# A delta-rule attention with a feed-forward behind it: T kept by columns in the head, and four moves of copies, loads and steps

## The chip, the cores and the metric

The kernel runs on one core of one Trainium2 chip. The metric is the device time of one execution in microseconds, as the median of several runs. TensorE (PE in the profile; PEld is its loading of weights), VectorE (DVE), ScalarE (ACT), GpSimd (POOL) and SyncE (SP, which here only issues DMAs) each work through a queue of their own, in order, and wait for one another by semaphores.

## What is computed

A linear attention with a delta rule runs over 768 steps for 4 sequences of 8 heads with 48 entries each. Its output, 3072 tokens of 384 entries, goes through a feed-forward layer of 2048 columns with a leaky ReLU.

```python
for t in range(S):
    y[:, :, t] = einsum('bhd,bhde->bhe', q_t, state)
    v_old = einsum('bhde,bhd->bhe', state, k_t)
    state = state + beta_t * einsum('bhd,bhe->bhde', k_t, v_t - v_old)
...
h = x @ w_in            # 384 -> 2048
g = maximum(0.01 * h, h)
out = g @ w_out         # 2048 -> 384
```

Here k_t is k divided by its norm.

## The kernel before, in words

The 768 steps are cut into 12 blocks of 64. Within a block the recurrence is a triangular system. `gram` makes the products of keys with keys and with queries, `inv` inverts the triangular matrix by elimination, `solve` puts its halves together (`merge_z`, tiles pz and zs; `merge_u`, tile pu, results in rt) and gets y from it (`step_w`, `step_y`, tile ys). `columns` turns y into x, and `ffn` runs the feed-forward of a block over 16 columns f of 128 hidden entries: the first products of f and f + 1 (tile ph, line 800), an activation on ScalarE, and PD = 2 columns later the second product (tile po, line 791). Heads and sequences are split into two groups g = 0, 1.

The inverses of blocks 0 and 1 are made together, ahead of everything else (`inv(0)`, where `two` is true): T is one tile of 32 by 32 entries on 128 partitions, T[p, m, i] with rows m. Step j of `eliminate` adds T[m, j] * L[j, i] to T[m, i] for all m up to j and all i behind j. Where both sides have more than ONE = 3, it does so with two products into tmp (line 407) and two sums (line 412), one pair for the even rows and one for the odd rows; else with single instructions (line 395). Behind the last step VectorE transposes T twice in blocks of 32 by 32: into tc (line 466), whose parts `place` copies into rt (line 516), and in place (line 472), from where `merge_u` takes it for blocks 0 and 1. `place(0, g, 1)` runs on ScalarE, `place(0, g, 0)` on VectorE.

Beside this, in the head, the weights come in eight loads of 1.5 MB (`load_w`, tile wr, tags w0 to w7). Each is taken apart into parts that TensorE multiplies: `pack` on ScalarE (line 148), `conv` on VectorE (lines 158 to 161), `expand` on ScalarE (line 168), `final` on VectorE (line 175). Block 0 works in plain 32 bits (`w32`), later blocks in two parts each (`cast`, `lows`).

What sets the order: a library plans each engine's order from a simulated timeline, and the kernel binds it where it matters. `behind(name)` puts an instruction behind the one last marked with that name on its engine. The mark `dv` chains the weight conversions on VectorE one behind the other, so that `final` of weight 1 comes behind `conv` of weight 2; `po` puts pz and pu of later blocks behind the last second product. From line 850 on generators are woven into the loop over f: SV[n] lists for block n the columns f behind which the next block's solve goes a step on, IV and G4 the same for its inverse and its Gram. `warm` keeps TensorE busy with products that nobody reads.

The inputs of block 2's Gram (tile kq, line 288, four DMAs of 192 KB on SP's queue) are asked for in the head. The inverse of block 3 goes to memory as tt and comes back as the tile sq (line 495), which pz of block 3 reads.

Of the kernel before, what the change touches and what calls it, by code (L numbers as in the profile page):

```python
# [9 lines left out]
F32 = mybir.dt.float32  # L10
# [5 lines left out]
ALU = mybir.AluOpType  # L16
# [4 lines left out]
D = 48  # L21
# [4 lines left out]
GS = 2  # L26
NGR = NSEQ // GS
# [3 lines left out]
HS = H * NSEQ  # L31
HC = C // 2
P = 128
# [10 lines left out]
R0 = 64  # L44
# [3 lines left out]
def delta_moe_kernel(ctx: ExitStack, tc, kq0, kqT, kv, qT, beta, cst, w_all, out, nblk):  # L48
# [73 lines left out]
    def behind(name):  # L122

        return tc.issue_after(mark[name]) if name in mark else nullcontext()
# [155 lines left out]
    def gram(n):  # L280
        need(sv, "y", n - Q_BUFS // NGR)
        kqs = []
        for g in range(NGR):
            t = sb.tile([P, GS, NPAIR, 2, C], F32, tag="kq", name=f"kq{n}_{g}", bufs=KQ_BUFS)
            kqs.append(t)
            with behind("L" if n > BG + 1 else "kq"), behind("A" if BG + 1 < n < 2 * BG + 2 else None):
                for b in range(2):
                    nc.sync.dma_start(t[b * R0:b * R0 + D].rearrange("p s u x t -> p (s u x t)"), kqT[n, g, b])
        if n == GS:
            yield  # L290
        b0 = where[n][0]
        Lh[b0] = sb.tile([P, HC, HC], F32, tag="L", name=f"L{b0}", bufs=2)
        gd = dr.tile([64, HC, HC], F32, tag="gd", name=f"gd{n}")
        queue = nc.gpsimd if n == GS * NGR else nc.sync
        for g in range(NGR):
            kq = kqs[g]
            gs = sb.tile([P, 2, NPAIR, C], F32, tag="gs", name=f"gs{n}_{g}", bufs=2)
            if not g:
                gm[n] = sb.tile([P, GU, HC], F32, tag="gm", name=f"gm{n}", bufs=GM_BUFS)

            ps = [ps_a.tile([P, 512], F32, tag="a", name=f"pg{n}_{g}_{b}") for b in range(2)]
            pv = [x.rearrange("p (u x t) -> p x u t", u=NPAIR, x=2) for x in ps]
            for p in range(NPAIR):
                for c in range(2):
                    for b in range(2):
                        r = slice(b * R0, b * R0 + D)
                        with behind("ph") if n > 2 else nullcontext():
                            nc.tensor.matmul(ps[b][c * 64:(c + 1) * 64, p * 128:(p + 1) * 128],  # L308
                                             kq[r, c ^ b, p, 0], kq[r, c ^ b, p].rearrange("p x t -> p (x t)"),
                                             start=True, stop=True)  # L310
            for b in range(2):
                nc.scalar.copy(gs[:, b], pv[b][:, 0])  # L312
            for c in range(2):
                for e in range(2):
                    a = e * HS + g * GH + c * GU
                    queue.dma_start(
                        gd[a:a + GU].rearrange("l j i -> j l i"),
                        gs[c * 64 + e * HC:c * 64 + (e + 1) * HC].rearrange("p b u t -> p (b u) t")[:, :, e * HC:(e + 1) * HC])

            def masked(pv=pv, qa=of("q", n, g), to=DATA[g]):  # L320
                for b in range(2):
                    for c in range(2):
                        r = slice(c * 64, (c + 1) * 64)
                        with behind("gl") if n > 2 else nullcontext():
                            nc.vector.tensor_tensor(  # L325
                                qa[to, c, b * NPAIR:(b + 1) * NPAIR], pv[b][r, 1],
                                tri[r].rearrange("p (o t) -> p o t", o=1).broadcast_to([C, NPAIR, C]), ALU.mult)

            def corners(g=g, gs=gs):
                for c in range(2):  # L330
                    k = 2 * g + c
                    with behind("h") if n > 2 else nullcontext():
                        (nc.scalar.copy if n > 2 else nc.vector.tensor_copy)(gm[n][k * HC:(k + 1) * HC].rearrange("p (b u) t -> p b u t", b=2), gs[c * 64:c * 64 + HC, :, :, HC:])

            if n == 2:
                masked()
                corners()
            elif not g:
                masked()
                held.append(corners)  # L340
            else:
                tails.extend([[masked], held + [corners]])
                held.clear()
            if g == NGR - 1:
                for r in range(2):
                    i = queue.dma_start(Lh[b0][r * 64:(r + 1) * 64].rearrange("l j i -> l (j i)"), gd.rearrange("l j i -> l (j i)"))
                if n == GS * NGR:
                    mark["kq"] = i.ins
                if n > GS:
                    mark["L"] = i.ins  # L350
                done.add((gram, n))
            yield
# [32 lines left out]
    def eliminate(b, L, j, T, m):  # L385


        w = HC - 1 - j
        gate = "xl" if b == 1 and j >= XL else None
        if min(m, w) <= ONE:  # L390
            rows = m <= w
            for x in range(min(m, w)):
                with behind(gate):
                    t = T[:, x, j + 1:] if rows else T[:, 0:m, j + 1 + x]
                    d = nc.vector.scalar_tensor_tensor(  # L395
                        t, L[:, j, j + 1:] if rows else T[:, 0:m, j],
                        T[:, x, j:j + 1] if rows else L[:, j, j + 1 + x:j + 2 + x], t, ALU.mult, ALU.add)
                mark["steps"] = mark[f"step{min(x, 1)}"] = d.ins
            return
        parts = []  # L400
        for x in range(min(m, 2)):
            t = T[:, x:m:2]
            k = t.shape[1]
            tv = sb.tile([P, 144], F32, tag=f"tmp{x}", name=f"tmp{b}_{j}_{x}", bufs=1)
            tv = tv[:, 0:k * w].rearrange("p (x w) -> p x w", x=k)
            with behind(gate):
                nc.vector.tensor_tensor(  # L407
                    tv, t[:, :, j:j + 1].broadcast_to([P, k, w]),
                    L[:, j, j + 1:].rearrange("p (o w) -> p o w", o=1).broadcast_to([P, k, w]), ALU.mult)
            parts.append((tv, t[:, :, j + 1:]))  # L410
        for x, (tv, t) in enumerate(parts):
            mark["steps"] = mark[f"step{x}"] = nc.vector.tensor_tensor(t, t, tv, ALU.add).ins  # L412
# [11 lines left out]
    def inv(b):  # L424
# [34 lines left out]
        for j in range(HC - 1):  # L459
            eliminate(b, L, j, T, j + 1 if two else j // 2 + 1)  # L460
            if two and j in WARM:
                warm(WARM[j], T[:, 0, j:j + 1])
            if j == HC - 2:
                if two:
                    Tc = sb.tile([P, HS, HC], F32, tag="L", name="tc", bufs=2)
                    nc.vector.transpose(Tc.rearrange("p l i -> p i l"), T.rearrange("p m i -> p i m"))

                    for i, n in enumerate(NB[b]):
                        Tts[n] = Tc, T[i * 64:i * 64 + HC]
                    for g in range(NGR):  # L470
                        place(0, g, 1)
                    d = nc.vector.transpose(T, T)
                    mark["inverse"] = d.ins
                    for g in range(NGR):
                        d = place(0, g, 0)
# [37 lines left out]
    def place(n, g, e):  # L513
        a = n * 64 + e * HC
        with behind("h" if n else "inverse"):
            return (nc.scalar.copy if e or n else nc.vector.tensor_copy)(
                half_of(n, g, e), Tts[n][0][a:a + HC].rearrange("p (y g u) i -> p g y u i", y=2, g=NGR)[:, g])

    squares = {}
# [117 lines left out]
    def solve(n):  # L637
# [88 lines left out]
        def step_y(g):  # L726

            qa, v = of("q", n, g), of("v", n, g)
            pv = ps_a.tile([P, 512], F32, tag="a", name=f"py{n}_{g}")
            for c, u, e in quarters():  # L730
                a = (c ^ (u // NPAIR)) * C + e * HC
                nc.tensor.matmul(pv[a:a + HC, u * D:(u + 1) * D], qa[:, c, u, e * HC:(e + 1) * HC], v[:, c, u], start=True, stop=True)  # L732
            ys[n, g] = y = sb.tile([P, DO], F32, tag="ys", name=f"ys{n}_{g}", bufs=3)
            mark["ys"] = nc.scalar.copy(y, pv[:, 0:DO]).ins
            if not n and not g:
                expand(0, "ys", slice(1, 2))

        slots = NSLOT - (n < EARLY)
# [158 lines left out]
    conv(1)  # L897
    expand(0, "rv", lo)
    final(0, lo)
    for j in (4, 5):  # L900
        load_w(j, "dv")
    weave(1, (sv, 2, 0, 1))
    next(gg)
    final(0, hi)
    work = {
        0: ((expand, 1, "xh"), (conv, 2)),
# [24 lines left out]


WEARLY, NPACK, NG = 4, 3, 5
WARM, FILL = {HC // 2: 28, HC - 2: 12}, dict(pz=2, pu=3)
KA = 2
BG = 2
ONE = 3
XL, IL = 24, HC - 1 - 24
IV, GG = ((9, 16), (6, 17), (2, 12), (2, 12)), ((2, 4), (1, 2))
G4 = (0, 1), (13, 14), (12, 13)  # L940
SV = (1, 2, 4, 5, 7, 12, 13), (4, 6, 7, 9, 11, 12), (2, 4, 5, 7, 9, 10), (3, 3, 5, 6, 8, 10, 11)
PD, FB = 2, 4


# [64 lines left out]
```

## Time and profile before

| | us |
|---|---|
| median of 3 runs | 593.85 |
| lowest, highest | 591.87, 595.17 |
| the profiled execution, time | 597.18 |
| the profiled execution, span | 595.4 |

| engine | busy us | share of the span |
|---|---|---|
| TensorE, matmuls | 565.9 | 95% |
| TensorE, weight loads | 520.0 | 87% |
| VectorE | 421.7 | 71% |
| ScalarE | 336.7 | 57% |
| GpSimd | 82.3 | 14% |

The profile is of one execution. Its times count from the start of the span. Busy shares are means over stages with different limits; the stages are told apart below by their time: the head up to 54 us, block 0's feed-forward up to 110, block 1's up to 162, and from there some 44 us for a block. The granted clock is that of TensorE: 1.00 is 2.4 GHz, 0.50 is 1.2 GHz.

### The profile page before, as it was taken

What the parts mean: (1) busy time and instruction counts of PE and PEld (TensorE: products, weight loads), DVE (VectorE), ACT (ScalarE), POOL (GpSimd) and SP (SyncE); (2) the same over time, 40 slices, a digit from 0 to 9 for tenths busy, and PEclk for the clock granted to TensorE, in tenths of its full rate; (3) what the DMA queues carried; (4) which work ended last, traced back from release to release, by engine and by line L of the source; (5) the groups of instructions that cost most, each with busy time, mean ns of one, the idle gap of its engine ahead of it and who ended that gap; (6) DMA issues with size and microseconds to landing.
All of it is one profiled execution on the core that took longest, in us unless ns stands there. A gap on an engine that the chain in (4) does not pass through costs nothing.

```text
span 595.4 us, 22234 instructions
## 1 busy us (share of the span) xinstructions
PE 565.9 (95%) x9137; PEld 520.0 (87%) x9137; DVE 421.7 (71%) x1788; ACT 336.7 (57%) x865; POOL 82.3 (14%) x143
## 2 busy tenths in 40 slices
PE   4588999989989999999999999999999999999996
PEld 4467777779879999999999999999999999999996
DVE  3998899969829769669669669579589489241221
ACT  3686989885536546545545545545555554454432
POOL 7000000130320030130310310310300400400100
PEclk9998999999989999999999999999999999999999
DMA  5994952272760390490590590591581640510101
GB/s 113 309 303 169 299 153 53 64 144 51 141 109 13 61 192 21 78 200 4 86 193 3 104 175 19 81 183 29 87 165 30 103 95 3 84 36 3 28 0 28
DMA packets 102502, 59.68 MB, mean 100 GB/s; under 512 B 90496, under 2 KB 91584, under 8 KB 101376
## 3 DMA queue, kind: packets, MB, share of 16 engines
q1 hardware_dynamic: 96992, 50.06, 39.0%
q0 software_dynamic: 4832, 7.48, 5.6%
q8 instruction: 72, 1.18, 0.9%
q10 hardware_dynamic: 576, 0.72, 0.6%
q14 instruction: 30, 0.25, 0.2%
HBM read 46.96 MB, written 11.27 MB: 98 GB/s over the span
## 4 chain that ended last, share of the span: by engine, by line
PE 74%; DVE 10%; ACT 7%; DMA 4%; issue 2%; SPq 1%; DVEq 0%; ACTq 0%
PE ph L800 29%; PE po L791 29%; PE pw L695 3%; ACT rv L630 2%; PE py L732 2%; PE pg L308 2%; DVE T L412 2%; DVE tmp L407 2%; PE pk L669 2%; PE pc L669 1%; PE px L767 1%; ACT cg L148 1%; DVE T L395 1%; DMA sq<-tt 1%; PE pz L534 1%
## 5 line engine op out<-in xcount | busy, mean ns | idle before, releaser
L791 PE MATMUL po<-w,gh 128*128 128x384 f32 x704 | 178.1, 343 | 0.0
L815 DVE TENSOR_TENSOR gl<-ph,gh 128x256 fp32r<-128x256 f32 x176 | 74.4, 423 | 139.7 <-ACT ph L814 136.3
L810 ACT ACTIVATE gh<-ph 128x256 fp32r<-128x256 f32 (+1 forms) x192 | 73.7, 385 | 175.9 <-PE ph L800 106.9
L800 PE MATMUL ph<-xh,w 128*128 128x256 f32 x1056 | 157.1, 285 | 0.0
L800 PEld LDWEIGHTS ph<-xh,w 128*128 128x128 f32 x1056 | 142.1, 191 | 4.1 <-issue 3.3
L791 PEld LDWEIGHTS po<-w,gh 128*128 128x128 f32 x704 | 120.4, 189 | 4.0 <-issue 1.6
L791 PE MATMUL po<-w,gl 128*128 128x384 f32 x352 | 112.2, 338 | 0.9 <-DVE gl L815 0.8
L800 PE MATMUL ph<-xl,w 128*128 128x256 f32 x528 | 91.0, 284 | 0.0
L412 DVE TENSOR_TENSOR T<-T,tmp 128x48 f32<-128x48 f32 (+12 forms) x490 | 87.8, 215 | 0.3
L407 DVE TENSOR_TENSOR tmp<-T,L 128x48 f32<-128x48 f32 (+12 forms) x490 | 87.5, 215 | 0.2
L800 PEld LDWEIGHTS ph<-xl,w 128*128 128x128 f32 x528 | 75.3, 192 | 0.3 <-issue 0.2
L791 PEld LDWEIGHTS po<-w,gl 128*128 128x128 f32 x352 | 65.3, 188 | 2.1 <-DVE gl L815 2.1
L814 ACT ACTIVATE ph<-ph 128x256 f32<-128x256 f32 x176 | 66.8, 380 | 0.0
L495 POOL DMA_DIRECT2D sq<-tt x36 | 21.2, 596 | 301.4 <-PE po L791 110.8
L842 POOL DMA_DIRECT2D out<-ob x44 | 23.3, 535 | 142.9 <-ACT ob L841 142.5
L325 DVE TENSOR_TENSOR rq<-pg,csb 64x256 f32<-64x256 f32 x80 | 33.8, 422 | 2.5 <-ACT gs L312 0.9
L680 ACT ACTIVATE rt<-pk 48x512 f32<-48x512 f32 x44 | 26.1, 593 | 6.4 <-PE pk L669 5.0
L697 ACT COPY rv<-pw 64x384 f32<-64x384 f32 x48 | 22.8, 475 | 3.5 <-PE pw L695 2.3
L791 PE MATMUL po<-cg,gh 128*128 128x384 f32 x64 | 23.1, 494 | 0.0
L800 PE MATMUL ph<-x,cg 128*128 128x256 f32 x96 | 22.3, 382 | 0.4 <-ACT x L772 0.4
L630 ACT ACTIVATE rv<-rv,nt 64x48 f32<-64x48 f32 x96 | 22.3, 318 | 0.2
L395 DVE SCALAR_TENSOR_TENSOR T<-L,T 128x27 f32<-128x27 f32 (+3 forms) x126 | 22.2, 242 | 0.0
(110 smaller groups left out, 657.6 us busy)
## 6 DMA issues: line engine op xcount, KB each, us to landing
wr<-in_w_all SPq DMA_DIRECT2D x8, 1536.0 KB, 13.8
kq<-in_kqT SPq DMA_DIRECT2D x40, 192.0 KB, 5.8
rv<-in_kv SPq DMA_DIRECT2D x24, 192.0 KB, 5.6
rk<-in_kv SPq DMA_DIRECT2D x24, 192.0 KB, 5.1
rq<-in_qT SPq DMA_DIRECT2D x24, 192.0 KB, 3.6
L<-gd SPq DMA_DIRECT2D x18, 256.0 KB, 4.4
out<-ob POOLq DMA_DIRECT2D x44, 96.0 KB, 4.4
td<-T SPq DMA_DIRECT2D x20, 128.0 KB, 3.2
```

The source lines that it names most:

```text
L325: nc.vector.tensor_tensor(qa[to, c, b * NPAIR:(b + 1) * NPAIR], pv[b][r, 1], tri[r].rearrange("p (o t) -> p o t", o=1).broadcast_to([C, NP ...
L395: d = nc.vector.scalar_tensor_tensor(t, L[:, j, j + 1:] if rows else T[:, 0:m, j], T[:, x, j:j + 1] if rows else L[:, j, j + 1 + x:j + 2 + ...
L407: nc.vector.tensor_tensor(tv, t[:, :, j:j + 1].broadcast_to([P, k, w]), L[:, j, j + 1:].rearrange("p (o w) -> p o w", o=1).broadcast_to([P ...
L412: mark["steps"] = mark[f"step{x}"] = nc.vector.tensor_tensor(t, t, tv, ALU.add).ins
L630: d = nc.scalar.mul(v[DATA[g], c, u], v[DATA[g], c, u], nt[DATA[g], g, c, u:u + 1])
L680: d = nc.scalar.mul(ts[g][STATE[g], c], pv[g][c * C:c * C + D].rearrange("p (y v) t -> p y v t", y=2), -1.0)
L791: i = nc.tensor.matmul(po[t][:, :DO], a[:, ts_], w, start=(f == 0 and k == 0), stop=(f == NFC - 1 and k + 1 == len(ways)))
L800: i = nc.tensor.matmul(ph, w[:, cc * P:(cc + 1) * P], a, start=(k == 0), stop=(k + 1 == len(ways)))
L810: i = nc.scalar.activation(gh, ph, AF.Prelu, alpha=0.01)
L814: i = nc.scalar.activation(ph, ph, AF.Prelu, alpha=0.01)
L815: mark["gl"] = mark[f"gl{n}_{f}"] = nc.vector.tensor_tensor(gl, ph, gh.bitcast(F32), ALU.subtract).ins
L842: nc.gpsimd.dma_start(out[r0:r0 + C], ob[a:a + C])
```

## The change

T of blocks 0 and 1 is kept by columns, T[p, i, m], and `eliminate` splits its columns m into a lower and an upper half in place of even and odd rows. The first transpose now reads T straight, the second reads it strided and writes into a tile of its own, G, which takes the place of weight 7 (tag w7). `place(0, 0, 1)` goes from ScalarE to VectorE, and the second transpose is put behind it. The second batch of warm matmuls has 7 in place of 12.

The loads of kq for block 2 wait for a copy of one column of ys into their tile, on GpSimd, and the mark `kq`, behind which weights are loaded, is on the last of them; the call that issues them and the loads of weights 4 and 5 change places accordingly. The second half of weight 0 is expanded behind y of g = 1, and no longer behind that of g = 0. SV[2], the steps of block 3's solve in block 2, becomes that of the later blocks without its first entry.

```diff
@@ gram
+            if n == GS:
+                nc.gpsimd.tensor_copy(t[:, 0, 0, 0, 0:1], ys[0, g][:, 0:1])
             with behind("L" if n > BG + 1 else "kq"), ...:
                 for b in range(2):
-                    nc.sync.dma_start(t[b * R0:b * R0 + D]..., kqT[n, g, b])
+                    i = nc.sync.dma_start(t[b * R0:b * R0 + D]..., kqT[n, g, b])
+            if n == GS:
+                mark["kq"] = i.ins
@@ eliminate
         parts = []
-        for x in range(min(m, 2)):
+        if not b:
+            for x, (lo, hi) in enumerate(((0, (m + 1) // 2), ((m + 1) // 2, m))):
+                tv = sb.tile([P, 144], F32, tag=f"tmp{x}", name=f"tmp{b}_{j}_{x}", bufs=1)
+                tv = tv[:, 0:(hi - lo) * w].rearrange("p (w x) -> p w x", w=w)
+                nc.vector.tensor_tensor(
+                    tv, T[:, j:j + 1, lo:hi].broadcast_to([P, w, hi - lo]),
+                    L[:, j, j + 1:].rearrange("p (w o) -> p w o", o=1).broadcast_to([P, w, hi - lo]), ALU.mult)
+                parts.append((tv, T[:, j + 1:, lo:hi]))
+        for x in range(min(m, 2) if b else 0):
@@ inv
-                    nc.vector.transpose(Tc.rearrange("p l i -> p i l"), T.rearrange("p m i -> p i m"))
+                    nc.vector.transpose(Tc.rearrange("p l i -> p i l"), T)
+                    G = sb.tile([P, 8 * DO], F32, tag="w7", name="turned", bufs=1)[:, 0:HC * HS].rearrange("p (m l) -> p m l", m=HC)
 
                     for i, n in enumerate(NB[b]):
-                        Tts[n] = Tc, T[i * 64:i * 64 + HC]
-                    for g in range(NGR):
-                        place(0, g, 1)
-                    d = nc.vector.transpose(T, T)
+                        Tts[n] = Tc, G[i * 64:i * 64 + HC]
+                    mark["placed"] = place(0, 0, 1).ins
+                    place(0, 1, 1)
+                    with behind("placed"):
+                        d = nc.vector.transpose(G, T.rearrange("p i m -> p m i"))
@@ place
-            return (nc.scalar.copy if e or n else nc.vector.tensor_copy)(
+            return (nc.scalar.copy if n or e and g else nc.vector.tensor_copy)(
@@ step_y
-            if not n and not g:
+            if not n and g:
                 expand(0, "ys", slice(1, 2))
@@ the order of the head
+    weave(1, (sv, 2, 0, 1))
+    next(gg)
     for j in (4, 5):
         load_w(j, "dv")
-    weave(1, (sv, 2, 0, 1))
-    next(gg)
@@ constants
-WARM, FILL = {HC // 2: 28, HC - 2: 12}, dict(pz=2, pu=3)
+WARM, FILL = {HC // 2: 28, HC - 2: 7}, dict(pz=2, pu=3)
-SV = ..., (2, 4, 5, 7, 9, 10), (3, 3, 5, 6, 8, 10, 11)
+SV = ..., (3, 5, 6, 8, 10, 11), (3, 3, 5, 6, 8, 10, 11)
```

Left out are the lines that only rename T's entries for the new order, in the single instructions of `eliminate` and in `warm`.

## Rows read from the trace of the kernel before

**Rows 1.** Busy time by stretch: stretch, length, busy (instructions) by engine, granted clock, DMA share, GB/s

```profile
36.67:58.12 21.45, 18.05 (x467) 14.36 (x468) 20.81 (x30) 15.34 (x28) 0.00 (x0) 0.84 0.63 184
...
54.00:110.00 56.00, 55.67 (x804) 42.09 (x805) 51.02 (x142) 51.11 (x93) 0.00 (x0) 1.00 0.61 180
...
172.00:173.00 1.00, 1.00 (x4) 1.00 (x4) 0.13 (x1) 0.83 (x3) 0.00 (x0) 0.50 1.46 130
...
175.00:176.00 1.00, 1.00 (x10) 1.00 (x8) 0.00 (x0) 0.00 (x0) 0.00 (x0) 0.83 0.00 0
...
210.00:254.00 44.00, 44.00 (x730) 41.64 (x729) 33.55 (x159) 23.16 (x62) 7.15 (x14) 1.00 0.50 96
```

**Rows 2.** Timeline of VectorE in the head: start, time, engine, line, operation, tiles, shapes, count

```profile
24.40 0.48 DVE L407 TENSOR_TENSOR tmp<-T,L 128x126 f32<-128x126 f32 x2
24.80 0.48 DVE L412 TENSOR_TENSOR T<-T,tmp 128x126 f32<-128x126 f32 x2
...
34.92 0.33 DVE L412 TENSOR_TENSOR T<-T,tmp 128x56 f32<-128x56 f32 x2
35.28 1.35 DVE L395 SCALAR_TENSOR_TENSOR T<-T,L 128x29 f32<-128x29 f32 x6
36.67 2.31 DVE L466 STREAM_TRANSPOSE tc<-T 128x1024 f32<-128x1024 f32 x1
39.09 1.25 DVE L472 STREAM_TRANSPOSE T<-T 128x1024 f32<-128x1024 f32 x1
40.36 0.86 DVE L516 COPY rt<-tc 32x512 f32<-32x512 f32 x2
...
56.36 1.75 DVE L175 SCALAR_TENSOR_TENSOR cg<-wr,cg 128x1536 uint32<-128x1536 uint32 x1
```

**Rows 3.** Timeline of TensorE, head and block 0

```profile
36.50 2.97 PE L421 MATMUL warm<-neg 128*128 128x512 f32 x12
...
58.60 2.86 PE L800 MATMUL ph<-x,cg 128*128 128x256 f32 x12
...
76.32 2.12 PE L584 MATMUL pu<-zs,T 32*32 32x32 f32 x64
```

**Rows 4.** Timeline of ScalarE, head and block 0

```profile
35.67 4.56 ACT L148 COPY cg<-wr 128x1536 bf16<-128x1536 bf16 x3
40.25 1.26 ACT L516 COPY rt<-tc 32x512 f32<-32x512 f32 x2
...
51.96 0.84 ACT L168 CAST cg<-cg 128x768 f32<-128x768 bf16 x1
...
62.80 1.61 ACT L148 COPY cg<-wr 128x1536 bf16<-128x1536 bf16 x1
...
91.54 1.67 ACT L148 COPY cg<-wr 128x1536 bf16<-128x1536 bf16 x1
```

**Rows 5.** Timeline of TensorE around its waits for sq, in brackets idle time before, and releaser

```profile
125.80 0.64 PE L534 MATMUL pz<-sq,gm 128*32 128x128 f32 x16 [1.56 <-DMA sq<-tt]
...
167.09 0.86 PE L791 MATMUL po<-w,gh 128*128 128x384 f32 x4
...
171.19 0.64 PE L534 MATMUL pz<-sq,gm 128*32 128x128 f32 x16 [2.89 <-DMA sq<-tt]
171.77 1.53 PE L791 MATMUL po<-w,gh 128*128 128x384 f32 x4
```

**Rows 6.** VectorE's groups by shape from 9 to 13 us: busy, mean ns, idle before

```profile
L250 DVE STREAM_TRANSPOSE L<-S 128x1024 f32<-128x1024 f32 x1 | 1.9, 1933 | 0.1
```

**Rows 7.** Timeline of SP's queue: issue, time to issue, count

```profile
24.77 7.01 SPq L288 DMA_DIRECT2D kq<-in_kqT  x4
...
65.17 0.33 SPq L133 DMA_DIRECT2D wr<-in_w_all  x1
```

**Rows 8.** Loads of weights, issue to landing: of 4 and 5, then of 7

```profile
DMA to landing us min/median/max: 6.1/8.8/11.6
...
DMA to landing us min/median/max: 15.2/15.2/15.2
```

More of the change, by code (lines that the diff above doesn't have):

```diff
@@ L285, in gram @@
             kqs.append(t)
+            if n == GS:
+                nc.gpsimd.tensor_copy(t[:, 0, 0, 0, 0:1], ys[0, g][:, 0:1])
             with behind("L" if n > BG + 1 else "kq"), behind("A" if BG + 1 < n < 2 * BG + 2 else None):
                 for b in range(2):
-                    nc.sync.dma_start(t[b * R0:b * R0 + D].rearrange("p s u x t -> p (s u x t)"), kqT[n, g, b])
+                    i = nc.sync.dma_start(t[b * R0:b * R0 + D].rearrange("p s u x t -> p (s u x t)"), kqT[n, g, b])
+            if n == GS:
+                mark["kq"] = i.ins
         if n == GS:
@@ L393, in eliminate @@
                 with behind(gate):
-                    t = T[:, x, j + 1:] if rows else T[:, 0:m, j + 1 + x]
+                    at = (lambda m, i: T[:, i, m]) if not b else (lambda m, i: T[:, m, i])
+                    t = at(x, slice(j + 1, HC)) if rows else at(slice(0, m), j + 1 + x)
                     d = nc.vector.scalar_tensor_tensor(
-                        t, L[:, j, j + 1:] if rows else T[:, 0:m, j],
-                        T[:, x, j:j + 1] if rows else L[:, j, j + 1 + x:j + 2 + x], t, ALU.mult, ALU.add)
+                        t, L[:, j, j + 1:] if rows else at(slice(0, m), j),
+                        at(slice(x, x + 1), j) if rows else L[:, j, j + 1 + x:j + 2 + x], t, ALU.mult, ALU.add)
                 mark["steps"] = mark[f"step{min(x, 1)}"] = d.ins
@@ L461, in inv @@
             if two and j in WARM:
-                warm(WARM[j], T[:, 0, j:j + 1])
+                warm(WARM[j], T[:, j, 0:1])
             if j == HC - 2:
@@ L940 @@
 G4 = (0, 1), (13, 14), (12, 13)
-SV = (1, 2, 4, 5, 7, 12, 13), (4, 6, 7, 9, 11, 12), (2, 4, 5, 7, 9, 10), (3, 3, 5, 6, 8, 10, 11)
+SV = (1, 2, 4, 5, 7, 12, 13), (4, 6, 7, 9, 11, 12), (3, 5, 6, 8, 10, 11), (3, 3, 5, 6, 8, 10, 11)
 PD, FB = 2, 4
```

## The prediction

> **What bounds the kernel now.** I read the busy time by stretch first [rows 1]. From 54 to 110 us TensorE is busy for 55.67 of 56.00 us, and from 210 on for all of 44.00: there every microsecond counts one for one, and nothing that ScalarE, VectorE or a DMA gains is worth anything. What can be won lies in the head, before TensorE runs without a gap, and in the stalls between. So two places matter. In the head I read VectorE's stretch from the first transpose to the last weight conversion before the second pair of first products: 20.81 of 21.45 us busy in 30 instructions [rows 1]. That is not an engine that waits. Its timeline [rows 2] ends this stretch with the final step of weight 1, 56.36 + 1.75 = 58.11; TensorE starts the products that read this weight at 58.60 [rows 3]. VectorE has 0.5 us of slack there, no more. ScalarE in the same head [rows 4] does three weight copies (35.67 + 4.56 = 40.23) and then, in the order of its queue, the two copies of rt at 40.25, though the first transpose had ended at 36.67 + 2.31 = 38.98. So the way through rt is held by ScalarE, and not by T. The second place is block 2 [rows 5]: pz of block 3 waits 2.89 us, from 168.30 to 171.19, for the DMA that fills sq, and after it the granted clock stands at 0.50, the 1.2 GHz level, until about 175.3 (the slice 175 to 176 shows 0.83) [rows 1].
>
> **T by columns, the elimination.** The number of instructions and of elements is the same: a step with m columns of T and w entries still makes two products and two sums of about m*w/2 elements. Runs of 28 and of 4 elements cost the same already (56 elements in 0.33 us a pair at the end of the loop [rows 2], 0.34 at its start), so I cost the new order of elements at nothing. What is new is who waits for whom. Before, rows of T were split into even and odd, and a row never changed its half; each instruction depends on the one two places ahead. Now the columns are split in the middle, and the middle moves: if m is even, the first half of the next step takes over one column of the second half of this one. Its product then reads what the instruction directly ahead has written. The price of that stands in [rows 2]: a pair that depends on nothing directly ahead starts 0.08 us before the earlier pair has ended (24.40 + 0.48 against 24.80), one that does starts 0.03 after (34.92 + 0.33 against 35.28). That is 0.11 us each, for m = 4, 6, ..., 26, twelve times: 1.3 us. Bounds: 0, if something can be put between, and 1.4.
>
> **The two transposes.** The first one reads and writes T strided by 128 bytes and takes 2.31, the second reads and writes without stride and takes 1.25 [rows 2]; the one of the start, strided reading alone, took 1.93 [rows 6]. Now the first reads straight and writes strided, which no row shows: between 1.25 and 2.31; I take 1.25 + (2.31 - 1.93) = 1.63. The second reads strided and writes straight, as the row with 1.93; bounds 1.25 and 2.31. Sum 3.56 before and 3.56 after, with bounds of -1.06 and +1.06.
>
> **rt's copy for one g on VectorE.** VectorE gets one copy more, 0.86 / 2 = 0.43 and 0.02 between [rows 2]: +0.45. ScalarE loses one of two, 1.26 / 2 = 0.63 [rows 4], and as that way starts at 40.25 whatever T does, pz for the second g starts 0.6 us earlier. The transpose into the new tile stands behind this copy on VectorE, but pu, its reader, needs zs first and has that cover.
>
> **The rest of the head.** The half of w that moves behind y of the second g is a cast of 0.84 on ScalarE [rows 4] that stands ahead of that y now: up to 0.84 won on the way to px, I take 0.6. Five of the twelve warm matmuls go, 5 x 2.97 / 12 = 1.2 us [rows 3]; they end ahead of pz in both kernels, so nothing. The four kq loads, asked for at 24.77 so far, and 7.01 us on SP's queue [rows 7], go behind a one-column copy on POOL that waits for ys. On SP they hold what is queued behind them: the loads of weights 4 and 5. Of these the first landed 6.1 us after its issue [rows 8], at 58.9, and ScalarE reads it at 62.80 [rows 4]. With four issues of 0.3 to 0.5 us and 0.8 MB ahead of it I reckon with 61 to 62: covered, with under 2 us to spare. If that cover went, ScalarE's queue would stand. The tile for the turned T has the place of weight 7, so that this load waits until pu of block 1 has read it, 76.32 + 2.12 = 78.4 [rows 3] in place of 65.17 [rows 7]; with the 15.2 us it took [rows 8] it lands by 93.6 at the latest, and with 6.1 us, for a queue as empty as weight 4 found it, by 84.5. Its reader starts at 91.54 [rows 4]. I take the early end, since 65 to 78 has been cleared of it, so nothing.
>
> **Sum for the head.** TensorE's and ScalarE's side gains 0.6 + 0.6 = 1.2. VectorE's side loses 1.3 + 0 + 0.45 = 1.75: the final step of weight 1 ends at 59.9, the products behind it start there, and not at 58.60: **+1.3 us**. With no slack up to 110 it stays.
>
> **Block 3's solve a step later.** In block 2, pz stands behind the second product of one more column, as long as the one that began at 167.09 and ended at 168.30: 1.2 us at most, 1.0 without its start. The DMA comes when it comes (its chain begins in block 1), so of 2.89 some 1.0 is filled and 1.9 us stay. The wait of 1.56 us at 125.80 [rows 5] left the granted clock at 1.00, so I take it that the clock stays up. Four matmuls of po took 1.53 us behind the stall and 0.86 ahead of it [rows 5]; over the 3.4 us to 175.3 this is 3.4 x (1 - 0.86 / 1.53) = 1.5. Together **-2.5 us**; bounds -1.0 (the clock falls all the same) and -4.4 (no wait left).
>
> **The whole** is +1.3 - 2.5 = -1.2 us. The profiled execution had a span of 595.4 and a time of 597.18, 3.3 above the median of the three runs; I apply the difference to the median: 593.85 - 1.2 = **592.6 us**. By the bounds of this case alone 590.9 to 594.5.
>
> **Rivals.** *The dependence costs nothing* (0.17). The wait is hidden, or something fits between. VectorE's loss is 0.45, which its slack covers: -2.5, 591.4. Against it stand the starts of [rows 2]. A rule of the Trainium skill leads here too: VectorE: DVE Perf Modes, in The DRAIN you can't avoid, says that the next operation starts when the pipeline is empty, and that eight copies took as long with a semaphore after each as with one at the end. By that this case would hold; the trace disagrees, since independent pairs overlap by 0.08 us.
>
> *The clock falls all the same* (0.14): -1.0 + 1.3 = +0.3, 594.2. For it: 1.9 us is nearer to 2.89 than to nothing. Against it: the row at 125.80.
>
> *VectorE gets shorter* (0.22): both transposes near 1.25 and no dependence, 0.45 - 1.06 = -0.6. Then TensorE's side decides with its 1.2, VectorE stands ready at 57.5, and the products start 1.1 earlier: -1.1 - 2.5 = -3.6, 590.3. The same time, within 0.6, comes if the stall goes wholly beside my head: +1.3 - 4.4 = -3.1. For it: 1.25 stands in the trace. Against it: strided access cost time in both rows that have it.
>
> *Halves taken as overlapping* (0.12), the slow side. Both halves now lie in the same rows of T, and if the dependence tracking compares whole stretches of memory, each second sum waits for the first, and each first product of the next step for the second sum: 2 x 25 waits of 0.11 = 5.5 us in place of 1.3. VectorE then ends at 58.11 + 5.5 + 0.45 = 64.1: +5.5 - 2.5 = +3.0, and +4.5 with the clock down: 596.9 to 598.4. It decides from the second sum of the first step on. Against it: interleaved rows lay in one stretch too, and did not wait.
>
> **How the numbers follow.** My case has 0.35; with the two rivals beside it that stay near, 0.66 lies within 0.5% (3.0 us, about what a measurement of this kernel can tell from no change). Faster by more is the third rival, 0.22, slower the fourth, 0.12. The range from 589.4 (no dependence and the whole stall gone, -4.4) to 596.3 takes in the bounds of the others; the slow rival and a tenth of the rest stay out.
>
> **What would show it.** The gap between the second sum of a step and the next product on VectorE: 0.03 us after its end at every other step, or the overlap as before. The transposes: 1.63 and 1.93. Final of weight 1 near 59.9 and the products directly behind it. In block 2, pz with a wait of about 1.9 us and a granted clock of 1.00 behind it. I am wrong if VectorE isn't what the products at 58.60 end up waiting for, if weight 4 or 7 lands after its reader is due, or if the wait for sq keeps its length.

## The result, and the profile of the changed kernel

The changed kernel takes **599.46 us** (median of six executions, 596.88 to 603.21), the kernel before 593.34 in the same runs: a ratio of **1.0108, 95% interval 1.0071 to 1.0146**. It is slower by 6.1 us, where 592.6 was forecast, and lies outside the range (589.4 to 596.3).

The profiled execution of the changed kernel has a span of 597.9 and a time of 599.66, near its median. That of the kernel before was 3.8 us above its own, as the table shows when a second profile of the same kernel (run e4 below) stands beside it. Times on TensorE, in us (px is the product that turns y into x; where nothing else is said, the start):

| point | before | before, second profile | after |
|---|---|---|---|
| px of the first pair ends | 53.89 | 53.46 | 51.19 |
| products of the second pair | 58.60 | 58.18 | 61.20 |
| px of block 1 | 107.50 | 107.11 | 113.74 |
| px of block 2 | 159.24 | 158.31 | 165.96 |
| px of block 3 | 207.37 | 201.95 | 209.64 |
| span | 595.4 | 590.0 | 597.9 |

Against the second profile the time is lost twice, between px and the products of the second pair (3.0 us behind there), and in the second half of block 0 (3.6 more); block 1 costs another 1.0. What block 2 gives back (165.96 to 209.64 is 43.68, before 48.13) the second profile of the kernel before has too, with the old positions (43.64).

TensorE's timeline of the changed kernel in the head, columns as in [rows 3], with the idle time before and its releaser in brackets:

```profile
50.05 1.14 PE L782 MATMUL px<-csb,ys 128*128 128x128 f32 x6
53.94 5.46 PE L815 MATMUL ph<-x,cg 128*128 128x256 f32 x12 [2.75 <-DVE wr L131]
...
61.20 2.86 PE L815 MATMUL ph<-x,cg 128*128 128x256 f32 x12
```

px is done 2.7 us earlier than in the profile before, more than the 1.2 I gave this side. But the products behind it wait for weight 0's first half, whose step on VectorE ends at 53.8 (the releaser named, a memset, stands right behind that step). Then twelve of them take 5.46 instead of 2.86. The stretches of the same kernel, columns as in [rows 1], name the cause, the granted clock in the third column from the end:

```profile
54.00:60.00 6.00, 6.00 (x28) 4.45 (x30) 4.91 (x7) 1.00 (x4) 0.00 (x0) 0.50 1.05 359
60.03:107.00 46.97, 44.57 (x751) 33.62 (x748) 40.00 (x83) 40.77 (x65) 0.00 (x0) 1.00 0.66 178
108.00:111.00 3.00, 3.00 (x8) 2.37 (x8) 3.00 (x24) 2.35 (x6) 0.00 (x0) 0.50 0.40 82
```

Twice in block 0 the clock stands at 0.50, the 1.2 GHz level, and both times TensorE had idled ahead of it: 2.75 us here, 2.40 at 106.78 (below). VectorE's timeline, against [rows 2]:

```profile
16.73 0.98 DVE L400 SCALAR_TENSOR_TENSOR T<-L,T 128x31 f32<-128x31 f32 x5
...
25.38 0.47 DVE L425 TENSOR_TENSOR T<-T,tmp 128x126 f32<-128x126 f32 x2
25.77 0.49 DVE L410 TENSOR_TENSOR tmp<-T,L 128x136 f32<-128x136 f32 x2
...
35.09 0.20 DVE L410 TENSOR_TENSOR tmp<-T,L 128x56 f32<-128x56 f32 x1
35.33 0.22 DVE L425 TENSOR_TENSOR T<-T,tmp 128x56 f32<-128x56 f32 x1
...
36.79 2.11 DVE L479 STREAM_TRANSPOSE tc<-T 128x1024 f32<-128x1024 f32 x1
38.94 0.42 DVE L531 COPY rt<-tc 32x512 f32<-32x512 f32 x1
39.39 1.95 DVE L487 STREAM_TRANSPOSE turned<-T 128x1024 f32<-128x1024 f32 x1
...
57.25 1.75 DVE L175 SCALAR_TENSOR_TENSOR cg<-wr,cg 128x1536 uint32<-128x1536 uint32 x1
```

The product at 25.77 is one of the twelve for which I had counted a wait: the lower half of a step with m = 15 (8 columns of 17 entries, 136), which takes over a column of the upper half of the step before. It starts 0.08 before the sums ahead of it have ended (25.38 + 0.47), so it does not wait. The order on VectorE shows why: the upper half of each step runs beside the lower half of the step before. The two sums at 25.38 have 126 and 119 entries, the lower half of the step with m = 14 (7 columns of 18) and the upper half of that with m = 15 (7 of 17), so that the column taken over was written a step earlier. Where an instruction does read what the one directly ahead has written, at the end of the loop, it still waits: the sum at 35.33 starts 0.04 after its product has ended (35.09 + 0.20). The loop starts at 16.73 and the first transpose at 36.79, 0.12 after [rows 2]; in the kernel before the loop starts here:

```profile
16.70 1.04 DVE L395 SCALAR_TENSOR_TENSOR T<-L,T 128x31 f32<-128x31 f32 x6
```

Weight 1's final step ends at 59.00, 0.9 later than in [rows 2] and 0.9 earlier than forecast. The products behind it still start only at 61.20.

The second loss is weight 7's load. SP's queue, VectorE, ScalarE and TensorE of the changed kernel, one fence each:

```profile
86.72 1.10 SPq L350 DMA_DIRECT2D L<-gd  x2
87.91 0.54 SPq L133 DMA_DIRECT2D wr<-in_w_all  x1
```

```profile
83.02 1.76 DVE L175 SCALAR_TENSOR_TENSOR cg<-wr,cg 128x1536 uint32<-128x1536 uint32 x1
84.79 1.75 DVE L329 TENSOR_TENSOR rq<-pg,csb 64x256 f32<-64x256 f32 x4
86.57 0.58 DVE L337 COPY gm<-gs 32x256 f32<-32x256 f32 x2
87.22 0.06 DVE L131 MEMSET wr<- 128x1 f32 x1
```

```profile
96.13 1.58 ACT L148 COPY cg<-wr 128x1536 bf16<-128x1536 bf16 x1 [2.18 <-DVE sr L374]
```

```profile
102.73 1.64 PE L722 MATMUL pc<-rv,rk 128*48 128x48 f32 x64
106.78 4.51 PE L815 MATMUL ph<-x,cg 128*128 128x256 f32 x12 [2.40 <-DVE cg L175]
```

pu had read G by 80.9. The load then still waited for a memset, which `load_w` chains behind the mark `dv` and which stands behind a mask, a copy and others in VectorE's order, and for the issues of L on SP. It was issued at 87.91 instead of 65.17 [rows 7] and took 8.1 us, so it landed at 96.0, and ScalarE reads it at 96.13 instead of 91.54 [rows 4]. The releaser in brackets, VectorE's sr, is nothing that this copy reads: the load is what came last. The last pair's products pay: 2.40 us of idle time, and 4.51 instead of 2.86 at the half clock.

### The profile page after: what moved, and what is told of

Read it like the earlier page. It is cut to its first block, busy times and chain, and to the rows that moved or that the text cites. A ratio compares the mean times of both kernels' runs of the same rounds, so it can differ in the third digit from the quotient of the medians.

```text
span 597.9 us, 22233 instructions
## 1 busy us (share of the span) xinstructions
PE 566.8 (95%) x9132; PEld 521.1 (87%) x9132; DVE 422.6 (71%) x1789; ACT 336.0 (56%) x864; POOL 82.6 (14%) x145
## 4 chain that ended last, share of the span: by engine, by line
PE 74%; DVE 12%; DMA 7%; ACT 3%; issue 2%; SPq 1%; DVEq 0%; ACTq 0%
PE ph L815 31%; PE po L806 30%; PE pg L312 2%; PE pw L710 2%; PE py L747 2%; DMA wr<-in_w_all 2%; DVE T L425 2%; PE pk L684 2%; DVE tmp L410 1%; DMA L<-gd 1%; DMA rk<-in_kv 1%; PE pc L684 1%; PE px L782 1%; PE pz L549 1%; PE pu L549 1%
## 5 line engine op out<-in xcount | busy, mean ns | idle before, releaser
L420 DVE TENSOR_TENSOR tmp<-T,L 128x60 f32<-128x60 f32 (+23 forms) x440 | 76.9, 211 | 0.2
L815 PE MATMUL ph<-x,cg 128*128 128x256 f32 x96 | 26.7, 436 | 5.1 <-DVE wr L131 2.8
L815 PEld LDWEIGHTS ph<-x,cg 128*128 128x128 f32 x96 | 20.5, 218 | 9.7 <-issue 3.0
```

Source lines behind the costliest of these rows:

```text
L420: nc.vector.tensor_tensor(tv, t[:, :, j:j + 1].broadcast_to([P, k, w]), L[:, j, j + 1:].rearrange("p (o w) -> p o w", o=1).broadcast_to([P ...
L815: i = nc.tensor.matmul(ph, w[:, cc * P:(cc + 1) * P], a, start=(k == 0), stop=(k + 1 == len(ways)))
```

## The experiments

Twelve kernels, each timed in rounds beside the kernel before; a ratio is to that. The times stand in this table, and what they mean behind it:

| run | kernel | median us | before | ratio (95%) |
|---|---|---|---|---|
| e1 | changed; T in weight 7's place, G in T's | 600.76 | 593.36 | 1.0120 (1.0092 to 1.0147) |
| e2 | changed; 9 warm matmuls behind px | 595.29 | 593.36 | 1.0025 (1.0006 to 1.0044) |
| e3 | before; new SV[2] alone | 592.94 | 593.36 | 0.9988 (0.9968 to 1.0008) |
| e4 | before, again | 592.85 | 593.36 | 0.9985 (0.9957 to 1.0012) |
| e5 | before; kq's loads behind y alone | 597.48 | 592.87 | 1.0064 (1.0043 to 1.0086) |
| e6 | changed; kq's loads early | 597.66 | 592.87 | 1.0066 (1.0042 to 1.0089) |
| e7 | changed; kq early, G swapped | 595.23 | 592.87 | 1.0028 (1.0008 to 1.0048) |
| e8 | as e7, with the 9 matmuls | 593.65 | 592.87 | 1.0006 (0.9989 to 1.0024) |
| e9 | before; kq at rt, new SV[2] | 593.86 | 592.57 | 1.0002 (0.9972 to 1.0032) |
| e10 | as e9, w's half and final step moved | 593.78 | 592.57 | 0.9987 (0.9952 to 1.0023) |
| e11 | before; T by columns alone | 593.59 | 592.57 | 0.9993 (0.9958 to 1.0028) |
| e12 | as e1, kq at rt | 595.53 | 592.57 | 1.0023 (0.9995 to 1.0052) |

**Weight 7's place (e1).** 

```diff
-  X = sb.tile([P, HC * HC], F32, tag="T", ...)
+  X = sb.tile([P, 8 * DO], F32, tag="w7", ...)[:, 0:HC * HC] if two else ...
-  G = sb.tile([P, 8 * DO], F32, tag="w7", ...)
+  G = sb.tile([P, HC * HC], F32, tag="T", ...)
```

> The changed kernel, but block 0's T lies in the place of weight 7 and the turned copy G in the place of T; nothing else. Theory A (weight 7's load, held back by G, costs the most): its load is issued near 65 to 75 us as before, pack 7 runs near 91 to 93, the 2.4 us wait of the products of the last pair in block 0 goes, and with it the granted clock of 0.5 at 108 to 111 us. That gives back 2.4 + 1.65 = some 4 us, and up to 5.5 if the wait of 2.93 at the Gram stage of block 1 shrinks to 1.56 and its clock holds: 594 to 595.5. Theory B (the head costs it all: clock at 53 to 60): time stays within 1 us of the changed kernel's 599.5, as a gap later in block 0 would only move.

Weight 7 is asked for at 69.79 again, its wait goes, and the kernel is no faster. Another wait has come, earlier; VectorE and TensorE of e1:

```profile
90.26 0.48 DVE L450 MEMSET T<- 128x512 f32 x1
96.10 0.19 DVE L369 TENSOR_SCALAR sr<-L 128x32 uint32<-128x32 uint32 x1 [5.35 <-DMA L<-gd]
```

```profile
92.33 1.58 PE L710 MATMUL pw<-rv,rt 128*32 128x48 f32 x128
98.02 4.54 PE L815 MATMUL ph<-x,cg 128*128 128x256 f32 x12 [4.11 <-DVE cg L175]
```

VectorE takes its work in order; the first step of block 2's inverse waits 5.35 us for L, and weight 6's final step stands behind it. L was asked for at 91.37, in the second profile of before at 84.43. Both theories had missed this one. The busy share of the DMA engines (second column from the end) of that profile of before, and then of e1, shows why:

```profile
72.00:78.00 6.00, 6.00 (x109) 4.80 (x108) 5.65 (x11) 5.20 (x10) 0.00 (x0) 1.00 1.03 299
78.00:84.00 6.00, 5.85 (x30) 3.90 (x30) 5.90 (x8) 5.08 (x9) 0.00 (x0) 1.00 0.41 94
```

```profile
44.00:52.00 8.00, 6.37 (x265) 5.03 (x263) 7.71 (x13) 5.32 (x12) 0.62 (x2) 0.77 0.08 18
...
72.00:78.00 6.00, 6.00 (x75) 4.58 (x74) 5.72 (x10) 5.90 (x10) 0.00 (x0) 1.00 1.05 201
78.00:84.00 6.00, 6.00 (x65) 4.85 (x62) 5.90 (x7) 4.42 (x7) 0.00 (x0) 1.00 0.99 260
```

From 54 to 78 the engines are full in the kernel before already. With four loads of kq moved in there, and the two of rq that stood behind them on SP's queue (32.32 before, 54.72 in the changed kernel), six of 192 KB in all, they stay full up to 84, and what is asked for in this stretch comes later. The link to L is SP's queue, which stands until earlier loads have landed; SP's two longest waits in e1 from 71 to 90 us (us in total, times, longest):

```profile
SPq L320 <- DMA wr<-in_w_all: 6.4, 1, 6.4
SPq L290 <- DMA wr<-in_w_all: 4.4, 1, 4.4
```

They end when weight 6 has landed, at 78.2, and weight 7, at 87.1; in that profile of before these landed at 72.2 and 80.6. Behind them on the queue stand the DMAs that write gd, from which L is read.

**The gap ahead of the first products (e2).**

```diff
         mark["px"] = i.ins
+        if not n:
+            warm(9, gate="px")
```

> The changed kernel with nine warm matmuls between the solve of the first pair and its first products, where TensorE stood idle for 2.75 us (51.2 to 53.9). Theory B (the idle time let the clock fall, and the products at half clock cost 2.6 us): granted clock 1.00 from 53 to 60, the first products of the first pair take 2.9 instead of 5.5, the products of the second pair start near 59.1 to 59.5 (bound by VectorE's final step that ends at 59.0) instead of 61.2: 1.7 to 2.1 us less, 597.4 to 597.8. Rival: the matmuls only move the gap, or the clock falls for another reason: 599.5 as the changed kernel. Weight 7 stays late in both.

4.2 us less, twice what was expected. TensorE of e2, and the stretch with its clock:

```profile
51.45 1.04 PE L782 MATMUL px<-csb,ys 128*128 128x128 f32 x6 [0.36 <-ACT ys L749]
52.25 2.33 PE L434 MATMUL warm<-neg 128*128 128x512 f32 x9
54.42 2.75 PE L817 MATMUL ph<-x,cg 128*128 128x256 f32 x12
...
58.75 2.86 PE L817 MATMUL ph<-x,cg 128*128 128x256 f32 x12
...
106.18 2.86 PE L817 MATMUL ph<-x,cg 128*128 128x256 f32 x12 [2.38 <-DVE cg L175]
...
111.45 0.82 PE L782 MATMUL px<-csb,ys 128*128 128x128 f32 x6
```

```profile
50.00:110.00 60.00, 56.37 (x893) 42.59 (x893) 52.15 (x124) 49.66 (x82) 1.00 (x2) 1.00 0.71 193
```

The clock stays at 1.00, and the second pair starts at 58.75, 2.45 earlier. But at the last pair only 0.60 of this is left (106.18 against 106.78): weight 7 sets its start in both kernels, and the wait for it is there as before (2.38). What comes on top is the clock behind that wait: the products take 2.86 and not 4.51, another 1.65, so that px of block 1 comes 2.29 earlier (111.45 against 113.74). The rest of the 4.0 us between the two spans (597.9 and 593.9) lies behind it, 0.94 of it in block 1, where pz waits 0.32 us for sq at 1.00, and in the changed kernel 2.93 with 0.50 behind it. Why the clock did not fall behind the wait of 2.38, when it did in the changed kernel behind 2.40, no run shows. It is not one execution alone: over the timed ones the mean granted clock is 0.990 to 0.997 in e2 and 0.978 to 0.988 in the changed kernel.

**Block 3's solve, and the kernel before (e3, e4).** e3 is before with the one tuple changed; e4 is before unchanged.

```diff
-SV = ..., (2, 4, 5, 7, 9, 10), ...
+SV = ..., (3, 5, 6, 8, 10, 11), ...
```

> The kernel before with only the new positions of block 3's solve (3, 5, 6, 8, 10, 11). The comparison of the two profiles says that the stall ahead of it (2.89 us) and the half clock behind it go wholly: 4.45 us less in block 2, so 589 against 593.4. My prediction said 2.5 less: 591. Rival: the stall is mostly a thing of the one profiled execution of the kernel before, which was 3.8 us above its median, and the timed runs gain little: 592.5 to 593.5.

> The kernel before itself, once more, for a second profile and for the spread. If the stall of 2.89 us before block 3's Gram products and the half clock behind it stand in this profile too, they belong to the kernel; if the clock stays up here and the span is 2 to 4 us shorter, the profile of before overstated what the change of positions can win. Time 593.4 within 1.5 us, ratio 1.000.

e3 gains 0.4 us by the medians, and its interval includes no gain at all. e4's TensorE tells why, against [rows 5]:

```profile
166.85 0.51 PE L791 MATMUL po<-w,gl 128*128 128x384 f32 x2
167.29 0.64 PE L534 MATMUL pz<-sq,gm 128*32 128x128 f32 x16
167.87 0.96 PE L791 MATMUL po<-w,gh 128*128 128x384 f32 x4
```

With the old positions pz waits for nothing here, and no half clock follows. The stall of 2.89 us stands in the slower of the two profiles alone, and by e3's interval the new positions are worth 0.3% of the median (1.9 us) at most.

**kq and weight 7, apart and together (e5 to e7).** e5 is before with the first hunk of the diff, on the loads of kq, and the changed order of the head; e6 is the changed kernel without these, e7 that with e1's edit as well. e5's edit, on before:

```diff
+            if n == GS:
+                nc.gpsimd.tensor_copy(t[:, 0, 0, 0, 0:1], ys[0, g][:, 0:1])
...
+            if n == GS:
+                mark["kq"] = i.ins
...
-    for j in (4, 5):
-        load_w(j, "dv")
     weave(1, (sv, 2, 0, 1))
     next(gg)
+    for j in (4, 5):
+        load_w(j, "dv")
```

> The kernel before with only the loads of kq for block 2's Gram moved behind y (with the order of the loads of weights 4 and 5 that goes with it). Theory C (the DMA engines are full from 54 to 78 us in the kernel before already, so that every byte moved in there makes all that is asked for later come later): the loads that feed block 2's inverse (L) land near 96 us instead of 89, VectorE, which takes its work in order, waits some 5 us for them, and TensorE waits some 4 us near 95 to 98 us: 597 to 598.5, and up to 1.7 more if the clock falls behind that wait. Rival (weight 7's load alone was at fault, and moving kq is free): its load is early here, so 593.4.

> The changed kernel with the kq loads of block 2's Gram back at their old place near 25 us; G stays in the place of weight 7. Theory C with weight 7 as a second cause: the DMA engines are freer, but weight 7's load is asked for at 85 to 88 all the same and lands 6 us later at 91 to 94, against a reader due at 91.5 to 93: of the 2.4 us wait of the last pair's products 0 to 2 stay. With the clock's 2.6 us in the head kept: 596 to 599. If kq is the whole cause: 595.5.

> The changed kernel with both undone: kq loads at the old place, and G in the place of T instead of weight 7's. Theory C: no wait of TensorE between 62 and 110 us, as in the kernel before; what is left is the head's half clock (2.6 us at 53 to 60): 595.5 to 596.5. If it stays above 598, neither kq nor weight 7 is what costs time there.

e5 loses 4.6 us by kq alone (0.4 to 0.9% by its interval). VectorE and TensorE of e5 show the wait of e1:

```profile
95.07 0.19 DVE L369 TENSOR_SCALAR sr<-L 128x32 uint32<-128x32 uint32 x1 [5.41 <-DMA L<-gd]
```

```profile
96.99 5.49 PE L804 MATMUL ph<-x,cg 128*128 128x256 f32 x12 [3.33 <-DVE cg L175]
```

e6 keeps the wait for weight 7 (2.38 us at 104.70, its load issued at 85.68): freer DMA engines do not help a load that is asked for so late. So there are two causes, and they don't add up. By the ratios, with G in T's place kq's move costs 0.9% (e7 to e1), with G in weight 7's 0.4% (e6 to the changed kernel); and G in weight 7's place costs 0.4% with kq early (e7 to e6) and nothing with kq late. The step from e6 to the changed kernel is not clear of the spread of the two. Weight 7's late load takes its bytes out of the full stretch and its place off SP's queue, and L comes in time (VectorE waits 0.18 for it in the changed kernel). In e7 no wait in block 0 is longer than 0.81 us, and what my prediction had in mind can be seen; TensorE of e7:

```profile
54.04 2.86 PE L811 MATMUL ph<-x,cg 128*128 128x256 f32 x12 [0.35 <-ACT x L783]
...
59.08 2.86 PE L811 MATMUL ph<-x,cg 128*128 128x256 f32 x12 [0.60 <-DVE wr L131]
```

The second pair waits for VectorE, 0.5 to 0.9 us later than in the two profiles of before. The clock did not fall in this execution; I had expected that it would, since px would be early. It is not: with kq early, px ends at 53.7.

**The rest of the loss (e8, e11).** e8 is e7 with e2's edit. e11 is before with the hunks on `eliminate` and the two transposes, G and T placed as in e1, both copies of rt on ScalarE; of its diff the transposes:

```diff
-  nc.vector.transpose(Tc.rearrange("p l i -> p i l"), T.rearrange("p m i -> p i m"))
+  nc.vector.transpose(Tc.rearrange("p l i -> p i l"), T)
...
-  d = nc.vector.transpose(T, T)
+  d = nc.vector.transpose(G, T.rearrange("p i m -> p m i"))
```

> As the run before it (kq early, G swapped), and nine warm matmuls in TensorE's gap ahead of the first products. Theory: all of the loss is accounted for by the kq loads, weight 7 and the clock in the head: 592.5 to 593.5, the time of the kernel before, since VectorE's chain (transposes +0.5, the added copy +0.45) sets the start of the second pair's products at 58.5 to 59.3. If T by columns cost time beside these three, 594.5 or more.

> The kernel before with T by columns alone (its turned copy in the place of T, T in the place of weight 7): no other part of the change. The elimination costs nothing, the two transposes 0.5 us more (4.06 for 3.56): VectorE's final step of weight 1 ends at 58.6, the second pair's products start at 58.7 to 59.0: 593 to 593.8. My prediction's 1.3 for the elimination would give 594.2 to 594.8.

Neither differs from before by more than can be measured. Weight 0's half behind y of g = 1, the copy of rt on VectorE and the seven warm matmuls had no run of their own; e8 has them all. e8 lies 0.2% under e7, by the matmuls alone, though e7's profile shows no half clock: over its timed executions e7's mean granted clock runs from 0.983 to 0.994, e8's from 0.987 to 0.995. In e11 the transposes take 2.14 and 1.95, and TensorE waits as forecast:

```profile
58.41 2.86 PE L810 MATMUL ph<-x,cg 128*128 128x256 f32 x12 [0.65 <-DVE wr L131]
```

**The bytes, not the place (e12), and two tries at a faster kernel (e9, e10).** In all three, loads of kq wait for rt's second half. These are two of the four, since the copy writes only the lower rows of the tile; in e12 the other two are asked for at 24.37 and 30.86.

```diff
-                nc.gpsimd.tensor_copy(t[:, 0, 0, 0, 0:1], ys[0, g][:, 0:1])
+                nc.gpsimd.tensor_copy(t[0:HC, 0, 0, 0, 0:1], tv(0, g)[BASE[g]:BASE[g] + HC, 0, 0, 0, HC:HC + 1])
```

e10 also moves w's half behind y of g = 1, and swaps two steps of the head:

```diff
-        0: ((expand, 1, "xh"), (conv, 2)),
-        1: ((final, 1), (pack, 3, "h0_0"), ...
+        0: ((expand, 1, "xh"),),
+        1: ((final, 1), (conv, 2), (pack, 3, "h0_0"), ...
```

> The changed kernel with G in the place of T (weight 7 asked for early) as in the first run, and the kq loads asked for near 44 us, where the DMA engines are idle, in place of 50. Theory C: what made L of block 2 late (5.35 us of VectorE, 4.11 of TensorE at 98 us) was 1.2 MB of loads in the full stretch from 50 to 78 us; from 44 on they lie ahead of it, L lands by 91, and TensorE has no wait over 1 us between 62 and 110: 4 us less than the first run's 600.8, 595.5 to 597, of which the clock's fall in the head still holds 1 to 2.6. Rival (the place of weight 7 or the order on SP's queue is at fault, not the bytes): 599 to 601.

> The kernel before with block 3's solve at the new positions and the kq loads of block 2's Gram asked for behind rt's second half (near 44 us; two of the four loads stay early, since only their tile's lower rows wait), in place of 25 or 50. In the kernel before the DMA engines are idle from 45 to 53 us; with the loads behind y they are idle from 40 to 50. Theory: the bytes fit in there, so nothing is late behind 54 us; and if the loads under way at 40 to 45 us are what lengthens TensorE's gaps ahead of y (issue, 0.6 to 0.9 us), px comes up to 1.1 us earlier as in the run with the loads behind y: 591.6 to 592.6. Rival (the bytes must lie ahead of 40 us, or the gaps have another cause): 593, or 595 and more if L of block 2 is late again.

> As the run before it, with w's half moved behind y of the second g, as in the change, and with the final step of weight 1 ahead of the four steps of weight 2's conversion on VectorE. Theory: with TensorE's side earlier by some 1 us, VectorE's final step (57.2 to 59.0) sets the start of the second pair's products; ahead of the conversion it ends near 56.5 to 57, so that these products start at 57 in place of 58.2 to 58.6, and this stays: 591 to 592. Rival: the conversion, now 1.7 us later, holds ScalarE's cast of weight 2, and the gap moves to the third pair: 592.5 to 593.5.

e12 shows that these loads make L late, and not weight 7's place, which is as in e1: with two of the four early, and the other two and rq's moved at 43 to 48, where the engines of e1 were idle, VectorE finds L there and TensorE waits 0.46 at 102.80. That is 5.2 us less than e1 by one edit. Their bytes and their places on SP's queue moved together; no run tells the two apart. VectorE of e12:

```profile
89.85 0.48 DVE L450 MEMSET T<- 128x512 f32 x1
90.25 0.12 DVE L369 TENSOR_SCALAR sr<-L 128x32 uint32<-128x32 uint32 x1
```

No kernel beats the one before. What e9 and e10 were to win went elsewhere: TensorE stops inside py, the product that gives y, for 1.94 and 2.55 us, in e12 for 2.79, put down to nothing that the profile names ("issue"). TensorE of e12, the DMA queues of its stretch from 47 to 48 us (packets, MB, share), and its stretches around it:

```profile
47.26 0.66 PE L747 MATMUL py<-rv,rq 128*32 128x48 f32 x38
50.71 1.57 PE L747 MATMUL py<-rv,rq 128*32 128x48 f32 x66 [2.79 <-issue]
```

```profile
q1 hardware_dynamic: 39, 0.09, 45.8%
q8 instruction: 1, 0.02, 8.3%
```

```profile
43.50:47.50 4.00, 4.00 (x151) 3.25 (x153) 3.87 (x7) 1.43 (x4) 0.17 (x1) 0.52 0.91 193
47.50:51.50 4.00, 1.21 (x79) 1.07 (x70) 3.88 (x7) 1.78 (x3) 0.00 (x0) 0.91 0.04 8
```

The packet of program code (queue 8) moves there as the data end; in e5, with the engines idle from 40 to 50, one moves at 46 to 47 and py has no such gap. So e10's idea, the final step ahead of the conversion, was not put to the test: px came too late for it (53.32, and VectorE waited 1.59 for ScalarE ahead of that step).

## Why the prediction was wrong

**The elimination, +1.3: wrong.** The loop takes 36.67 - 16.70 = 19.97 in the kernel before and 36.79 - 16.73 = 20.06 in the changed one. The price of 0.11 for reading what the instruction directly ahead has written was right and still shows at the loop's end (35.33); the twelve places where I counted it are not there, since the order on VectorE has something between. That was my lower bound of 0, "if something can be put between", and a rival at 0.17. The page that I set against it (the Trainium skill, VectorE: DVE Perf Modes, The DRAIN you can't avoid) gives the right sum of nothing, though not for its reason, since the pairs still overlap by 0.07.

**The transposes, 0: a size.** The second took 1.95, near the forecast 1.93. The first, reading straight and writing strided, took 2.11 and not 1.63: strided writing costs 0.86 over 1.25, more than strided reading with 0.7. The sum is 4.06, +0.5. **rt's copy, +0.45: right** (0.42). **VectorE ends later: right**, by 0.9 and not 1.75.

**"The products behind it start there": wrong in the changed kernel**, right in e7 and e11. This is the first step that failed. I let TensorE's and ScalarE's gain vanish in a slack, as if time won on the side that doesn't bind cost nothing. It turned into an idle time of 2.75 us ahead of the first pair, the clock fell, and the second pair started 2.2 us after VectorE was ready for it. I had asked of the stall in block 2 whether the clock would fall behind it, and not of the gap that my own sum made: the first pair's x would have been there at 54.24 - 1.2 = 53.0, and weight 0's first half, which ends near 52.8 in the profile before (51.84 + 0.95), 1.75 later at 54.5. e2 puts 2.45 us on this at the second pair, 0.60 of them still there at the last pair. The gain itself, +1.2, was mis-sized too: with kq early there is none (px ends at 53.7 in e7, with stops of 1.20 and 1.19 us in TensorE's pw and py, against 53.46 and 53.89 before), and the 2.3 to 2.7 of the changed kernel show only with kq's loads late, which alone, in e5, give 0.7 to 1.1.

**Weight 7, nothing: wrong.** The lifetime was read rightly (pu is G's last reader), but not how the place is handed on: by a memset in VectorE's order and an issue in SP's. The issue came 9.5 us after the 78.4 that I took, 2.5 of them from the later head, and the load missed its reader. I had named this as a thing that would make me wrong.

**kq behind y, nothing: wrong.** I asked who stands behind the four loads on SP's queue, and found weights 4 and 5 covered; in the changed kernel they are (in e2 ScalarE waits 1.10 for weight 4, so the cover was as thin as said). I did not ask what the bytes do in a stretch where the DMA engines are full, nor that rq's loads go along, nor that SP's queue stands until earlier loads have landed. The sum of [rows 1], 0.61 from 54 to 110, hid it: an average over a full half and an empty one. e5 prices it at 4.6 us, as much as e2 does the gap.

**Block 3's solve, -2.5: wrong.** The mechanism may be right, but e4 has no such stall and e3 gains 1.9 us at most. The profiled execution had stood 3.3 us above the median, and I carried the gain over to the median whole. A time that far above the median is a reason to ask which of its stalls the median has.

**The rival on the slow side** had the sign and not the mechanism: no wait between halves stands in the trace. Two of the three things I named as proof against me came true, the cause of the second pair's start and weight 7.

The bounds of my case, 590.9 to 594.5, do not follow from its terms either: with the head at +1.3 they give 590.8 to 594.2, and the transposes' own bounds are not in them.

The account: filling the gap gives back 4.2 of the 6.1 us (e2); in its profile 0.60 of this is still the head's own, and 1.65 and 0.94 come from two later waits behind which the clock holds. 1.9 are left, with the wait for weight 7 (2.38) still in them. e8, with kq, weight 7 and the gap mended, has no loss that can be measured. That the causes overlap is shown by e1 and e6; an exact share for each does not exist.

## What to carry to other kernels

Ask of a load that is moved not only who stands behind it on its queue, but how full the DMA engines are, slice by slice, where its bytes will land, and what else is issued behind it. Ask of time won on an engine that does not bind where it will stand idle, and whether the clock falls there: a few matmuls in the gap were worth 4.2 us here. Ask of a gain in a profile whether it is still there behind the next wait: of 2.45 us 0.60 were. And where a profile is slower than the median, don't take a stall from it for the kernel's before a second profile has it too.

## What the chip showed that was not expected

**The clock behind a wait.** It fell behind waits of TensorE of 2.40, 2.75 and 2.93 us in the changed kernel, of 2.38 in e6, and of 1.94 inside py in e9 (0.50 from 50.6 to 53.9). It held behind 2.38 in e2, 2.29 in e7 and 2.56 ahead of pz in e5, and behind 1.56 in [rows 5]. Between 1.94 and 2.56 us it went both ways.

**Code loading behind data.** The gap in TensorE's py is 0.63 to 1.19 us wherever the loads of kq are early and the data end at about 45 (0.94 and 0.63 in the two profiles of before); none in e2 and e5, 0.47 in the changed kernel and 0.59 in e1, where the DMA engines are nearly idle from 40 on; 1.94 to 2.79 in e9, e10 and e12, with data from 43 to 48. In each of the twelve profiles with such a gap TensorE goes on 1.3 to 1.5 us after a packet of queue 8 has ended. The Trainium skill (Runtime: NRT & Kernel Launch, Instruction fetch mechanics) says that an engine's code comes in blocks by a DMA queue of its own, at a cost that is mostly hidden. The trace agrees on the queue and not on the cost, up to 2.79 us beside data traffic. That the late code is the cause is argued from the times of the packets; no run changed it alone.

**Transposes of 128x1024 on VectorE.** 1.25 us straight, 1.93 to 1.97 reading strided, 2.07 to 2.14 writing strided, 2.29 to 2.31 with both.
